# Re-tuning the planner of an attention-plus-MoE kernel: a larger reserve for DMA landings, and new order constants

## The chip, the cores and the metric

The kernel runs on one core of one Trainium2 chip. The metric is the device time of one execution in microseconds (us), lower is better. Its matrix engine is called PE here (PEld is its weight load), the vector engine DVE, the scalar (activation) engine ACT, the engine for memsets and cross-partition reductions POOL, and the queue that issues nearly all transfers SP.

## The reference

Eight batches of eight attention heads. Each sequence has 32 global and 512 local positions of 64 values. Global queries look at everything; local ones look at the global keys and at a band of 32 positions to either side. The attention output of all 4352 tokens then goes through a two-layer network with a Mish activation.

```python
s_g  = scale * q_g @ concat(k_g, k_l).T ;  out_g = softmax(s_g) @ v_all
s_ll = where(|i - j| <= 32, scale * q_l @ k_l.T, -1e9)
out_l = softmax(concat(scale * q_l @ k_g.T, s_ll)) @ concat(v_g, v_l)
x = concat(out_g, out_l) as (8 * 544, 512)
h = x @ w_in                 # 512 x 2048
g = h * tanh(log1p(exp(h)))  # Mish
return g @ w_out             # 2048 x 512
```

## The kernel before, in words

**Numbers as pairs.** Most matrix products run in 16-bit floats, with each operand split into a high and a low half, and three products (high-high, high-low, low-high) summed in PSUM. So most tiles come as a "hi" copy, made by ACT or DVE (line 347 on ACT, 349 on DVE), and a "lo" rest, which only DVE makes. The two weight matrices arrive as 64-bit floats in 32 half blocks of 512 KB. DVE rebuilds 32-bit floats from their bits in three instructions per half block (lines 426, 428, 435), PE squares them for a norm (`w_stat`, line 454, into the tile `w_s`), and a short chain over DVE, POOL and ACT turns the norm into a scale (`w_norm`, lines 461 to 474, tile `wp`, result `sw`). After that each of 16 weight blocks is split: hi by ACT or DVE, lo by DVE (line 486).

**Attention.** A unit is one batch `b`, one pair of heads `hp` and one quarter `t` of the sequence: 128 units. In each, PE makes two score tiles `s` (line 676 in 32-bit for the first eight head pairs, line 683 after that), DVE masks them and takes the row maximum (line 689), ACT exponentiates (line 698), ACT or DVE and then DVE split the result to `ph` (line 750). For batch 0 PE transposes it; from batch 1 on the DMA does (`pt<-ph`, line 509). Then PE multiplies by the values into `U` (line 767), whose normalised sum is `x` (line 777). The values reach the partitions where `U` needs them in seven small transfers per head pair (`va`, `vc`).

**Network.** There are 17 blocks of 256 tokens with 8 steps each. A step of the first product writes `h` (24 matmuls of 256 columns, line 899), ACT makes Mish out of it (`e`, line 942, with a table that must be loaded when the last function was an exponential), DVE splits it to `G` (lines 349 and 955), and a step of the second product adds it to `o` (12 matmuls of 512 columns, line 967). Two PSUM banks hold `h`, so a third step can start only when Mish has emptied the first.

**Who sets the order.** Each piece of work is a task with an engine (or a choice of two), a duration, what it reads and writes, and a priority. The class `Plan` simulates the five engines with these durations, always takes the task that can start first, and the simulated order is the order in which each engine's instructions are issued; nothing is reordered on the chip. A transfer's task is done, for the planner, at the time `served` at which its bytes have gone through, plus 400 ns, plus a reserve: `SPARE` when it is issued after the plan's time `SPARE_T`. Tasks of the weights get their due time as a place (`slot`) among the units: `CONV1`, `RATE1`, `CONV2`, `RATE2` for the conversions, `FIRST1`, `STEP1`, `FIRST2`, `STEP2` for the splits, `AHEAD_DMA` for the loads. `LEAD0`, `PACE` and `TAIL` say at which unit each network step is put; `LATE_*` postpone some loads and batch 1's preparation.

**Fillers.** The planner models that PE's clock is halved when the stretch of 3.4 us before had too few columns. Until the first `o` it therefore puts in matmuls that compute nothing which is used (line 1195, `w_s<-consts`, 256 columns). It does so where PE would wait at least `SLACK` longer than the filler takes, or where a debt stands: each task that uses few rows of the array adds its duration times `BOOST` to the debt, and a debt is paid in fillers whether PE would wait or not. In both cases it stops when the current stretch has `TARGET` columns.

Of the kernel before, what the change touches and what calls it, by code (L numbers as in the profile page):

```python
# [51 lines left out]
class Plan:  # L52
# [6 lines left out]
    DMA_IN, DMA_OUT, DMA_DEPTH = 1500, 400, 5500  # L59
    TICK, COLUMNS, PHASE = 10240 / 3, 3200, 0  # L60
    LOYAL = 800
    SLACK = 9.408
    TARGET = 5179.472
    SPARE_T = 148519.765
    BOOST = 0
    SPARE = 474.406
    TABLE = 1283

    def __init__(self):
# [75 lines left out]
    def order(self):  # L145
# [9 lines left out]
        start, done, on = [None] * N, [0] * N, [None] * N  # L155
        columns = {}
        served, spare, debt, last = 0, True, 0, 1
# [38 lines left out]
        for _ in range(N):  # L196
            t, pri, e, n, ns = min(c for c in map(first, free) if c)
            if any(tag == "o" for tag, _ in self.tasks[n][4]) and n != self.filler[0]:
                spare = False
            if e == PE and spare and done[self.filler[0]]:  # L200
                z, rows = max(free[PE], done[self.filler[0]] + self.HOP[DMA][PE]), self.tasks[n][6]
                while rows > last / 2 and columns.get(int((z + self.PHASE) / self.TICK), 0) < self.TARGET and (
                        debt > 0 and rows > 0.5 or tensor(z, self.filler[1], 1, False) + self.SLACK <= t):
                    z = tensor(z, self.filler[1], 1)
                    debt = max(0, debt - self.filler[1])
                    self.fill[n] = self.fill.get(n, 0) + 1
                t = max(t, z) if n in self.fill else t
                debt += ns * max(0, 1 - rows) * self.BOOST
                last = rows
            start[n], on[n] = t, e  # L210
            if e == ACT:
                self.table = self.tasks[n][7] or self.table
            for x, _ in self.tasks[n][0]:
                queue[x] = [c for c in queue[x] if c[1] != n]
            if e == PE:
                ns = tensor(t, ns, self.tasks[n][6]) - t
            if e == DMA:
                issue, ns = ns[:2]
                free[e] = t + issue + max(0, served - t - self.DMA_DEPTH)
                served = max(served, t + self.DMA_IN) + ns  # L220
                done[n] = served + self.DMA_OUT + (self.SPARE if t > self.SPARE_T else 0)
            else:
                free[e] = done[n] = t + ns
            for u in users[n]:
                left[u] -= 1
                if not left[u]:
                    enter(u)
# [17 lines left out]
def attn_mish_kernel(ctx: ExitStack, tc: tile.TileContext, qt, kt, qt0, kt0, mxs, vm, vg, qg, w1, w2, consts_in, out, w64):  # L245
# [80 lines left out]
    def bulk(kib):  # L326
        return dma(kib) + (BULK,)

# [664 lines left out]
        UNITS[:16] = sorted(UNITS[:16], key=lambda x: (x[2] // 2, x[1], x[2]))  # L993
    steps = [(blk, i) for blk in range(NBLK) for i in range(NF)]

    LEAD0 = 20.957
    PACE = 0.887
    TAIL = 14
    M1S = []
    for s in range(len(steps)):  # L1000
        at = int(LEAD0 + PACE * s) if s < 2 * NF else s + TAIL
        if s % NF == 0 and steps[s][0] < 2 * B:
# [136 lines left out]
                g_split(b + 1)  # L1139


    BULK = 4939.749
    LAG = 8
    ORDER = "k0 q0 m b k1 q1 w0 w1 g w3 w2 k2 q2 w4 w5 w6 w7 k3 q3 w8 w9 w10 w11 w12 w13 w14 w15"
    CONV1 = -2
    RATE1 = 1.119
    CONV2 = 0.367
    RATE2 = 1.486
    FIRST1 = 9.219
    STEP1 = 1.048  # L1150
    FIRST2 = 18.957
    STEP2 = 1.572
    AHEAD_DMA = 5.543
    LATE_K = 185.137
    LATE_L = 190.5
    LATE_B = 0
    LATE_V = 106.565

    def weights():
        for k in range(32):  # L1160
            at = CONV1 + RATE1 * k if k < 16 else CONV2 + RATE2 * (k - 16)
            if k >= 16:
# [22 lines left out]
    V.memset(pmax, 0.0)  # L1185
    for x in ORDER.split():
        a, n = x[0], int(x[1:] or 0)
# [94 lines left out]
```

## Time and profile before

| | |
|---|---|
| median of 3 runs | 954.24 us (954.09 to 954.46) |
| the profiled execution | 955.77 us, span 954.0 us |
| mean granted PE clock | 0.995 |
| PE busy | 919.7 us (96%) |
| DVE busy | 668.0 us (70%) |
| ACT busy | 629.0 us (66%) |
| DMA packets' time | 61.2% of 16 engines |

A row of the groups reads: line, engine, operation, output<-input, shape, count, then busy time and mean duration of one, then the idle time just before them. Matmul rows overlap, so their mean duration is longer than the distance between two of them; that distance is read from the chain of waits.

### The profile page before, as it was taken

The numbers are of one execution on the slowest core, as the hardware profiler recorded it, in microseconds if no ns is written. First come the engines' busy times: TensorE is split into PE (matmuls) and PEld (weight loads), VectorE is DVE, ScalarE is ACT, GpSimd is POOL, SyncE is SP. The second block draws the span as 40 slices with busy tenths as digits, with TensorE's granted clock in tenths as the row PEclk, the third lists the DMA queues.
The fourth block names the chain that finished last, engine by engine and source line by source line (L and its number), as shares of the span: only waits on it lengthen the run. The fifth ranks groups of instructions, "written<-read, shape, count | busy, mean of one in ns | idle before, by whom it ended". The sixth has DMA issues, their size and how long they took to land.

```text
span 954.0 us, 21026 instructions
## 1 busy us (share of the span) xinstructions
PE 919.7 (96%) x8181; PEld 641.5 (67%) x8181; DVE 668.0 (70%) x1771; ACT 629.0 (66%) x1284; POOL 16.2 (2%) x28
## 2 busy tenths in 40 slices
PE   7999999999999999999999999999999999999995
PEld 4666776557777777676777766677767776666663
DVE  6799988978999899767877777777766653222221
ACT  4557766778877898777886888687867881212110
POOL 2000000000000000000000000000000000000000
PEclk9999999999999999999999999999999999999998
DMA  9897446979998999756776576656765531000000
GB/s 305 266 292 219 117 143 150 203 154 241 242 250 194 263 217 197 160 125 142 168 169 129 138 164 161 131 142 148 167 120 110 94 77 24 23 2 23 1 23 23
DMA packets 214012, 141.04 MB, mean 148 GB/s; under 512 B 176664, under 2 KB 188184, under 8 KB 212888
## 3 DMA queue, kind: packets, MB, share of 16 engines
q1 hardware_dynamic: 213912, 139.69, 61.2%
q8 instruction: 64, 1.05, 0.5%
q14 instruction: 36, 0.29, 0.1%
HBM read 75.15 MB, written 8.91 MB: 88 GB/s over the span
## 4 chain that ended last, share of the span: by engine, by line
PE 75%; DVE 10%; DMA 8%; ACT 3%; SPq 2%; issue 2%; POOL 0%; DVEq 0%; ACTq 0%
PE h L899 31%; PE o L967 30%; DMA pt<-ph 5%; PE U L767 4%; PE s L683 3%; PE s L676 2%; PE g L807 2%; PE gu L856 1%; PE w_s L1195 1%; DVE W L428 1%; SPq L336 1%; DVE P L689 1%; DVE W L435 1%; SPq L509 1%; DVE ph L750 1%
## 5 line engine op out<-in xcount | busy, mean ns | idle before, releaser
L967 PE MATMUL o<-W,G 128*128 128x512 f16 x1632 | 390.9, 380 | 2.1 <-ACT W L347 1.1
L899 PE MATMUL h<-xh,W 128*128 128x256 f16 x2048 | 374.7, 273 | 0.1
L899 PEld LDWEIGHTS <-W 128*128 128x128 f16 x3264 | 311.0, 98 | 62.6 <-issue 6.0
L899 PE MATMUL h<-xl,W 128*128 128x256 f16 x1024 | 279.0, 272 | 0.0
L967 PEld LDWEIGHTS <-G 128*128 128x128 f16 x1632 | 156.8, 98 | 148.5 <-issue 5.8
L942 ACT ACTIVATE e<-h,c 128x512 f32<-128x512 f32 (+1 forms) x137 | 90.9, 682 | 124.8 <-PE h L899 118.8
L349 DVE TENSOR_SCALAR G<-e,c 128x512 f16<-128x512 f32 (+1 forms) x115 | 55.2, 480 | 149.1 <-ACT e L942 149.0
L698 ACT ACTIVATE P<-P,nm 128x192 f32<-128x192 f32 (+1 forms) x256 | 117.8, 461 | 48.0 <-DVE nm L689 45.0
L955 DVE SCALAR_TENSOR_TENSOR G<-e,c,G 128x512 f16<-128x512 f32 (+1 forms) x137 | 101.7, 743 | 2.3
L689 DVE CUSTOM_DVE_ANT_0 P<-s,consts 128x192 f32<-128x192 f32 (+1 forms) x256 | 90.7, 362 | 15.2 <-PE s L683 9.4
L750 DVE SCALAR_TENSOR_TENSOR ph<-P,ph 128x448 f16<-128x448 f32 (+1 forms) x112 | 65.0, 583 | 45.4 <-ACT ph L347 44.5
L942 ACT ACT_TABLE_LOAD x60 | 77.0, 1283 | 1.8 <-PE h L899 0.8
L698 ACT ACT_TABLE_LOAD x56 | 71.8, 1283 | 1.0
L767 PEld LDWEIGHTS <-pt 96*128 96x128 f16 (+1 forms) x1536 | 60.7, 97 | 14.7 <-DMA pt<-ph 9.6
L347 ACT ACTIVATE ph<-P 128x384 f16<-128x384 f32 (+1 forms) x108 | 58.7, 546 | 7.2 <-DMA pt<-ph 5.0
L767 PE MATMUL U<-va,pt 128*128 128x64 f16 (+1 forms) x768 | 55.1, 193 | 6.9 <-DMA pt<-ph 6.7
L767 PE MATMUL U<-vc,pt 96*128 96x64 f16 x768 | 54.9, 192 | 0.0
L683 PEld LDWEIGHTS <-qs 128*128 128x128 f16 x384 | 35.5, 98 | 23.1 <-issue 1.5
L698 ACT ACTIVATION_READ_ACCUMULATOR P<-P,nm 128x1 f32 x256 | 47.9, 187 | 0.0
L683 PE MATMUL s<-ks,qs 128*128 128x192 f16 (+1 forms) x192 | 42.7, 253 | 0.6 <-ACT gP L829 0.6
L829 ACT ACTIVATE gP<-g,gmx 64x288 f32<-64x288 f32 x64 | 30.3, 475 | 19.5 <-DVE gmx L824 19.4
L683 PE MATMUL s<-kl,qs 128*128 128x192 f16 (+1 forms) x192 | 42.6, 252 | 0.0
(125 smaller groups left out, 958.5 us busy)
## 6 DMA issues: line engine op xcount, KB each, us to landing
kraw<-in_kt SPq DMA_DIRECT2D x24, 640.0 KB, 4.7
kn_m<-in_mxs SPq DMA_DIRECT2D x24, 544.0 KB, 5.0
qraw<-in_qt SPq DMA_DIRECT2D x24, 512.0 KB, 4.5
out<-ob SPq DMA_DIRECT2D x34, 256.0 KB, 2.6
vraw<-in_vm SPq DMA_DIRECT2D x8, 1024.0 KB, 6.1
wraw<-in_w SPq DMA_DIRECT2D x16, 512.0 KB, 6.9
W<-in_w SPq DMA_DIRECT2D x16, 512.0 KB, 5.9
vc<-vf SPq DMA_DIRECT2D x32, 128.0 KB, 2.4
```

Of the source, the lines that this page charges most:

```text
L347: A.activation(out=dst, in_=src, func=AF.Copy, scale=c)
L349: V.tensor_scalar(dst, src, c, None, ALU.mult)
L683: T.matmul(X[s][:, :w], X[qs][:, h, t * 128:(t + 1) * 128], X[k][:, h, c0:c0 + w], start=(i == 0), stop=(i == 1))
L689: pl.add(DVE, 69 + 1.04 * w, lambda: V.tensor_tensor_reduce(out=X[P][:, h, :w], in0=X[s][:, :w], in1=mask[:, m0:m0 + w], scale=-SCALE, sca ...
L698: pl.add(ACT, 94 + 0.832 * w + 186, lambda: A.activation(out=X[P][:, h, :w], in_=X[P][:, h, :w], func=AF.Exp, bias=X[nm], scale=-1.0, accu ...
L750: pl.add(DVE, dve(n), lambda: V.scalar_tensor_tensor(p_part(X[ph], t, 1), p_src(X[P], t), PSC, p_part(X[ph], t, 0), ALU.mult, ALU.subtract ...
L767: T.matmul(X[u][:, t, h, :], X[pt][:k, p * 4 + h * 2 + c, :], X[vx][:k, t, vl, h * 64:(h + 1) * 64], start=(n == 0), stop=(n == 5))
L829: pl.add(ACT, 464, lambda part=part, c0=c0, c1=c1: A.activation(out=X[P][:, c0:c1], in_=X["g", b, hp, part][:64, 0:c1 - c0], func=AF.Exp, ...
L899: T.matmul(X[h][:, f * TB:(f + 1) * TB], wh(i, wl)[:, off:off + 128], X[x][:, d, o:o + TB], start=(n == 0), stop=(n == 11))
L942: chain(blk, i, ACT, 587, lambda a, z: A.activation(out=X[e][:, a:z], in_=hv(blk, i)[:, a:z], func=AF.Mish, bias=0.0, scale=X[c][:, 0:1]), ...
L955: chain(blk, i, DVE, 663, lambda a, z: V.scalar_tensor_tensor(gp(1, blk, i)[:, a:z], X[e][:, a:z], X["c", blk][:, 2:3], gp(0, blk, i)[:, a ...
L967: T.matmul(X[o], gp(g, blk, i)[:, f, t * 128:(t + 1) * 128], wh(8 + i, wl)[:, f * 512:(f + 1) * 512], start=(i == 0 and n == 0), stop=(i = ...
```

## The change

One rule and a set of constants change; no operation of the reference's computation is added or taken away.

```diff
-    SLACK = 9.408
-    TARGET = 5179.472
-    SPARE_T = 148519.765
-    BOOST = 0
-    SPARE = 474.406
+    RESERVE = 900
+    SLACK = 580.912
+    TARGET = 5641.608
+    SPARE_T = 42922.55
+    BOOST = 1.114
+    SPARE = 1474.111
...
-                done[n] = served + self.DMA_OUT + (self.SPARE if t > self.SPARE_T else 0)
+                done[n] = served + self.DMA_OUT + (self.RESERVE if t > 230000 else self.SPARE if t > self.SPARE_T else 0)
...
-    LEAD0 = 20.957
-    PACE = 0.887
-    TAIL = 14
+    LEAD0 = 18.646
+    PACE = 1.215
+    TAIL = 19
...
-    BULK = 4939.749
+    BULK = 5052.75
-    ORDER = "k0 q0 m b k1 q1 w0 w1 g w3 w2 k2 q2 w4 w5 w6 w7 k3 q3 w8 w9 w10 w11 w12 w13 w14 w15"
+    ORDER = "k0 q0 m b k1 w0 q1 w1 g w3 w2 q2 w4 k2 w5 q3 w6 w7 k3 w9 w10 w15 w11 w8 w13 w14 w12"
...
-    RATE2 = 1.486
-    FIRST2 = 18.957
-    STEP2 = 1.572
+    RATE2 = 1.396
+    FIRST2 = 24.578
+    STEP2 = 2.285
...
-    LATE_K = 185.137
-    LATE_L = 190.5
-    LATE_B = 0
+    LATE_K = 36.919
+    LATE_L = 293.152
+    LATE_B = 100.998
```

The reserve of a transfer is now 1474 ns when the plan issues it between 42.9 and 230 us, and 900 ns after that; it was nothing before 148.5 us and 474 ns after that. `DMA_OUT` (400 ns) comes on top in both. The fillers get a debt, and rise from 193 to 312; 287 of them stand ahead of the first `h`, where 192 did. All line numbers after line 61 are larger by one in the changed kernel. Four hi copies move from ACT to DVE, and ACT's table loads rise from 121 to 126.

How the order moves is shown at three places. The first is PE at the start: the score tiles of batch 0 (`s_0_0_t_head`), then before:

```order
L676 MATMUL s_0_0_0_0_110<-kn_0_0_93,qn_0_0_95 128x192
L676 MATMUL s_0_0_0_1_115<-kn_0_0_93,qn_0_0_95 128x192
L676 MATMUL s_0_0_1_0_121<-kn_0_0_93,qn_0_0_95 128x224
L676 MATMUL s_0_0_1_1_126<-kn_0_0_93,qn_0_0_95 128x224
L722 MATMUL T_0_0_0_133<-consts_65,P0_74 128x128 x4
L676 MATMUL s_0_0_2_0_145<-kn_0_0_93,qn_0_0_95 128x224
```

and now:

```order
L677 MATMUL s_0_0_0_0_109<-kn_0_0_93,qn_0_0_95 128x192
L677 MATMUL s_0_0_0_1_114<-kn_0_0_93,qn_0_0_95 128x192
L677 MATMUL s_0_0_1_0_121<-kn_0_0_93,qn_0_0_95 128x224
L677 MATMUL s_0_0_1_1_128<-kn_0_0_93,qn_0_0_95 128x224
L1196 LDWEIGHTS consts_65
L1196 MATMUL w_s_97<-consts_65 128x256
```

Thirteen fillers now stand before the first transposition `T`; before, the first filler came after 16 norm matmuls of `w_stat`, behind the first scores of head pair 1.

The second place is PE at the first step of the second product, `o_0_0`. The names are `h_block_step`. Before:

```order
L899 MATMUL h_1_2_1831<-xl_0_501,W_72 128x256
L899 LDWEIGHTS W_72
L899 MATMUL h_1_2_1831<-xh_0_451,W_72 128x256
L967 LDWEIGHTS G_0_1536
L967 MATMUL o_0_0_1893<-W_72,G_0_1536 128x512
```

and now:

```order
L900 MATMUL h_0_7_1864<-xl_0_571,W_72 128x256
L900 LDWEIGHTS W_72
L900 MATMUL h_0_7_1864<-xh_0_520,W_72 128x256
L968 LDWEIGHTS G_0_1593
L968 MATMUL o_0_0_1920<-W_72,G_0_1593 128x512
```

On DVE the first split of a second-matrix block (line 486, now 487) is followed by one reduction and the next split; before, 25 other instructions lay between those two. Eleven whole steps of `h` (264 matmuls) stood ahead of the first `o`; now eight (192) do. The rest of PE's work ahead of it is the same in number, apart from the fillers.

The third place is ACT around the norm of the second weight matrix (`wp_1`; the names `e_block_step` are Mish, `vf` and `vgf` the values of batch 1, and `W` the hi copy of a weight block). Before:

```order
L586 ACTIVATE vgf_1_1778<-vgraw_1_203,sv_1_1756 128x128
L347 ACTIVATE vf_1_0_1782<-vraw_1_929,sv_1_1756 128x4x128
L347 ACTIVATE vf_1_1_1785<-vraw_1_929,sv_1_1756 128x4x128
L942 ACTIVATE e_0_7_1803<-h_0_7_1700,c_0_1100 128x512
L347 ACTIVATE G_3_1776<-e_0_7_1803,c_0_1100 128x512
L942 ACTIVATE e_1_0_1824<-h_1_0_1763,c_1_1557 128x512
L347 ACTIVATE G_4_1828<-e_1_0_1824,c_1_1557 128x512
L467 ACT_TABLE_LOAD
L467 ACTIVATE wp_1_1735<-wp_1_1735 128x1
L468 ACT_TABLE_LOAD
L468 ACTIVATE wp_1_1735<-wp_1_1735 128x1
L347 ACTIVATE W_72<-W_72,sw_70 128x1024
```

and now:

```order
L943 ACTIVATE e_0_3_1716<-h_0_3_1634,c_0_952 128x512
L830 ACT_TABLE_LOAD
L830 ACTIVATE gP_1_0_1750,gs_1_0_1751<-g_1_0_0_1595,gmx_1_0_1647 64x288
L468 ACT_TABLE_LOAD
L468 ACTIVATE wp_1_1725<-wp_1_1725 128x1
L699 ACT_TABLE_LOAD
L699 ACTIVATE P2_76,sums_1_1_1761<-P2_76,nm_1_1_0_0_1731 128x192
L469 ACTIVATE wp_1_1725<-wp_1_1725 128x1
L587 ACTIVATE vgf_1_1767<-vgraw_1_257,sv_1_1753 128x128
...
L348 ACTIVATE W_72<-W_72,sw_70 128x1024
L943 ACT_TABLE_LOAD
```

The norm's two functions stand ahead of batch 1's values now, and ahead of the fifth Mish step of block 0 where they followed the first step of block 1.

More of the change, by code (lines that the diff above doesn't have):

```diff
@@ L1139, in slot @@
                 g_split(b + 1)
-    BULK = 4939.749
+    BULK = 5052.75
     LAG = 8
-    ORDER = "k0 q0 m b k1 q1 w0 w1 g w3 w2 k2 q2 w4 w5 w6 w7 k3 q3 w8 w9 w10 w11 w12 w13 w14 w15"
-    CONV1 = -2
-    RATE1 = 1.119
-    CONV2 = 0.367
-    RATE2 = 1.486
-    FIRST1 = 9.219
-    STEP1 = 1.048
-    FIRST2 = 18.957
-    STEP2 = 1.572
-    AHEAD_DMA = 5.543
-    LATE_K = 185.137
-    LATE_L = 190.5
-    LATE_B = 0
-    LATE_V = 106.565
+    ORDER = "k0 q0 m b k1 w0 q1 w1 g w3 w2 q2 w4 k2 w5 q3 w6 w7 k3 w9 w10 w15 w11 w8 w13 w14 w12"
+    CONV1 = 0.868
+    RATE1 = 0.869
+    CONV2 = 0
+    RATE2 = 1.396
+    FIRST1 = 11.002
+    STEP1 = 1.007
+    FIRST2 = 24.578
+    STEP2 = 2.285
+    AHEAD_DMA = 4.214
+    LATE_K = 36.919
+    LATE_L = 293.152
+    LATE_B = 100.998
+    LATE_V = 116.143
     def weights():
```

## The prediction

> **What bounds the kernel now.** I read the page's busy shares first, then PE in stages of the span, then the fillers in the same stages, and last what DVE and PE waited for in each.
>
> ```profile
> span 954.0 us, 21026 instructions
> PE 919.7 (96%) x8181; PEld 641.5 (67%) x8181; DVE 668.0 (70%) x1771; ACT 629.0 (66%) x1284; POOL 16.2 (2%) x28
> ```
>
> PE's useful work is the same in both kernels. So the time is that work, plus fillers, plus PE's gaps, plus what follows its last matmul, and only the last three can change. The stages (columns: busy us of PE, PEld, DVE, ACT, POOL; clock; DMA):
>
> ```profile
> core 0: us, PE busy (x) PEld busy (x) DVE busy (x) ACT busy (x) POOL busy (x), PEclk, DMA share, GB/s
> 0.00:32.30 32.30, 24.62 (x97) 15.25 (x98) 23.80 (x75) 12.06 (x36) 6.79 (x13) 1.00 0.86 278
> 32.30:100.10 67.80, 61.22 (x653) 45.04 (x651) 60.72 (x167) 45.81 (x117) 0.49 (x1) 1.00 0.89 259
> 100.10:133.40 33.30, 32.83 (x296) 27.75 (x296) 31.51 (x77) 24.23 (x46) 0.71 (x2) 1.00 0.40 116
> 133.40:142.30 8.90, 6.88 (x35) 3.69 (x34) 6.78 (x23) 5.48 (x7) 1.06 (x1) 0.81 0.57 176
> 142.30:230.00 87.70, 84.69 (x767) 53.52 (x766) 74.64 (x188) 61.99 (x144) 0.35 (x1) 1.00 0.83 180
> 230.00:800.00 570.00, 565.50 (x5364) 400.43 (x5362) 434.30 (x1182) 454.73 (x900) 6.85 (x10) 1.00 0.71 160
> 800.00:944.00 144.00, 143.96 (x982) 95.80 (x980) 35.50 (x62) 24.61 (x36) 0.00 (x0) 1.00 0.03 12
> 944.00:954.00 10.00, 0.00 (x0) 0.00 (x0) 0.75 (x1) 0.04 (x1) 0.00 (x0) 0.65 0.17 52
> ```
>
> The same stages for `w_s` alone (fillers and norm matmuls):
>
> ```profile
> 0.00:32.30 32.30, 8.25 (x49) 0.00 (x0) 1.00 0.86 278
> 32.30:100.10 67.80, 30.80 (x249) 0.29 (x1) 1.00 0.89 259
> 100.10:133.40 33.30, 2.50 (x25) 0.29 (x1) 1.00 0.40 116
> ```
>
> Until 100 us PE has 14.3 us of gaps, and 39 us go to `w_s`: DVE sets the pace there (60.72 of 67.80 us). From 100.1 us, the first `h`, to 133.4 us PE is full. It loses 2.0 us around the first `o`, more for a halved clock, then 3.0 us to 230 and 4.5 us to 800. After that nothing is lost until the last 10 us, the same tail in both kernels. So the change can act at four places: before the first `o`, right behind it, up to 230 us, and up to 800 us.
>
> **The change part by part.**
>
> *The three deferred steps.* The order shows eight instead of eleven `h` steps ahead of the first `o`, other useful work being equal. Two pieces of the chain give what a step costs:
>
> ```profile
> 259.27 1.31 PE h L899 x12
> 262.41 2.59 PE o L967 x12
> ```
>
> A step has 24 matmuls: 2.62 us; three are 7.86 us, which must now be done later. At an unchanged start of the first `o` the end would move by **+7.9 us**. The start, however, hangs on DVE and ACT:
>
> ```profile
> 124.45 0.29 DVE L461 CUSTOM_DVE_ANT_0 wd<-w_s,consts 128x128 f32<-128x128 f32 x1 [0.18 <-PE w_s L454]
> 131.15 1.28 ACT L467 ACT_TABLE_LOAD   x1
> 134.19 0.15 DVE L353 TENSOR_SCALAR wp<-wp 128x1 int32<-128x1 int32 x1 [1.70 <-ACT wp L468]
> 135.95 1.28 DVE L486 SCALAR_TENSOR_TENSOR W<-W,sw 128x1024 f16<-128x1024 f32 x1 [0.91 <-ACT W L347]
> 135.97 0.38 PE L967 MATMUL o<-W,G 128*128 128x512 f16 x1 [1.08 <-ACT W L347]
> 137.29 4.08 PE L967 MATMUL o<-W,G 128*128 128x512 f16 x11 [0.94 <-DVE W L486]
> ```
>
> The second norm starts at 124.45 us and its scale is used from 134.8 us on, because ACT reaches the logarithm only at 131.15 us. Now that function stands ahead of the fifth Mish step, so the scale comes early, and the two waits of DVE (1.70 and 0.91 us) fall away. DVE's rows ahead of the first split of a second-matrix block are the same as before by line and count, less three `G` lo's:
>
> ```profile
> L955 DVE SCALAR_TENSOR_TENSOR G<-e,c,G 128x512 f16<-128x512 f32 (+1 forms) x137 | 101.7, 743 | 2.3
> ```
>
> That is 3 x 0.743 = 2.2 us. Waits and rows together make 4.8 us. But the order now has a table load (1.28 us in the rows above) and an exponential between the norm's two functions, and Mish waits behind the hi copy, so I count 3.0 of them: the first `o` at about 133.0 us. The part comes to 7.9 - 3.0 = **+4.9 us**. Its lower end is what DVE can save at most, its waits between 10 and 136 us:
>
> ```profile
> DVE P L689 <- PE s L676: 3.3, 4, 1.4
> DVE x L777 <- PE U L767: 3.2, 1, 3.2
> DVE vmx L524 <- DMA vraw<-in_vm: 2.5, 1, 2.5
> DVE wp L353 <- ACT wp L468: 1.7, 1, 1.7
> DVE W L486 <- ACT W L347: 0.9, 1, 0.9
> ```
>
> Without the one for `vraw`, whose load keeps its place, they are 9.1 us; with the 2.2 us the part would be 7.9 - 11.3 = -3.4. The upper end is no earlier start at all, +7.9, or more if fillers delay DVE (a rival).
>
> *The fillers.* 119 more, each 109 ns (the 24 matmuls of a step have the same 256 columns): 13.0 us. Up to 133.4 us PE was busy for 24.62 + 61.22 + 32.83 = 118.7 us; less the 7.9 of the deferred steps and with these 13.0 it is 123.8 us in 133. They fit, and I cost them at nothing; DVE's work is the cover. But the debt's fillers stand in front of score tiles without regard to a gap. If all were uncovered they would cost 13.0 us. On the other side they may bring something:
>
> ```profile
> 25.11 2.55 PE L1195 MATMUL w_s<-consts 128*128 128x256 bf16 x11
> 59.08 1.69 PE L1195 MATMUL w_s<-consts 128*128 128x256 bf16 x14
> ```
>
> Eleven fillers took 2.55 us at 25 us, fourteen only 1.69 us at 59 us: PE ran at half speed at first. With thirteen of them from the fifth instruction on it should be fast sooner. This helps only where DVE waits for PE, at most the 3.2 us for `U` and part of the 3.3 us for score tiles, and is inside the lower end above. The Trainium skill ("TensorE: Matmul & The Clock Gate", Part 1) says that one busy window of about 3.4 us releases the clock; by that rule the fillers free it some 20 us earlier and the sum would be up to 3.2 us lower; the rows fit the rule, but do not show when thirteen fillers suffice.
>
> *Right behind the first `o`.* The stage from 133.4 to 142.3 us has a granted clock of 0.81, and eleven `o` matmuls took 4.08 us where 11/12 of 2.59 are 2.37: 1.7 us, and the wait of 0.94 us for DVE's lo is on top. In the changed order only one reduction lies between the first two splits on DVE, so I take the wait to go; whether the clock stays up depends on PE's gaps just before. I take **-2.0 us** (0 to -2.7).
>
> *The reserve, 142 to 230 us.* What PE waits for there, then what its weight loads wait for, then the same from 230 to 800 us:
>
> ```profile
> PE U L767 <- DMA pt<-ph: 2.9, 3, 1.1
> PEld L767 <- DMA pt<-ph: 4.1, 3, 1.6
> PE U L767 <- DMA pt<-ph: 3.9, 5, 1.6
> PEld L767 <- DMA pt<-ph: 5.5, 6, 1.9
> ...
> DMA to landing us min/median/max: 3.0/3.3/8.0
> ```
>
> Nearly the whole gap of the stage (3.0 us) is `U` waiting for a transposed `pt` that landed late. The plan now puts `U` at least 1.0 us later against its `pt` (1474 less 474), with other matmuls between. Three waits of at most 1.1 us on PE: almost all go. I take **-2.5 us**; bounds -3.0, and +1.0 if the deferred `h` steps make new waits for the late Mish.
>
> *The reserve, 230 to 800 us.* Five waits, 3.9 us, of the 4.5 us lost. The reserve grows by 0.426 us, so five times that, 2.1 us, is the most that is moved out of the way by it alone; a landing of 8.0 us against a median of 3.3 is far outside it. I take **-1.5 us**, bounds -4.5 (every gap of the stage) and +1.5 (the late landings meet another order as badly).
>
> *Copies and tables.* Four hi copies go to DVE, five table loads of 1.28 us come on ACT, 6.4 us in all. From 230 us on PE is full (565.50 of 570) while ACT is busy 454.73; this hides them. Without cover they would cost 6.4 us.
>
> **Sum.** 4.9 - 2.0 - 2.5 - 1.5 = -1.1 us, from 955.77 us of the profiled execution to 954.67. That execution is 1.53 us above the median of the runs, so by the median: **953.1 us**. About 0.2% (1.9 us) is what a measurement of this kernel can tell from no change; this forecast lies inside it.
>
> **The rivals.**
>
> *A: faster, 949.9 us.* The early fillers wake PE's clock, and DVE's waits for `U` and scores shrink by half (-3.2 of 6.5), all else as above: 953.1 - 3.2. For it: eleven fillers in 2.55 us, and DVE at 60.72 of 67.80, so each DVE wait counts. Against: the plan puts the first `x` right behind its last conversion, so some wait for `U` stays. The rule of the Trainium skill above ("TensorE: Matmul & The Clock Gate", Part 1) speaks for this case.
>
> *B: slower, 958.3 us.* The debt's fillers lie on the path. Most score tiles of batch 0 come behind some of them on PE, which takes them in order; DVE's row maximum follows the scores, and DVE sets the pace. 95 of the 119 stand ahead of the first `h`: 10.4 us; if half is uncovered, 5.2 us come to the sum: 953.1 + 5.2 = 958.3. It decides from the point where DVE's waits for `s` exceed the 3.3 us of now. Against: DVE has conversions to do in between, and PE has 14.3 us of gaps to fill.
>
> *C: the reserve does not do what it says, 956.1 us.* If the late landings are later than the reserve covers, the 2.5 fall to 1.0 and the 1.5 to 0: 953.1 + 3.0 = 956.1. For it: the landing of 8.0 us against a median of 3.3. Against: the single waits from 142 to 230 us were at most 1.1 us on PE, about what the reserve grows by.
>
> **How the numbers follow.** The forecast (951.0 to 955.2) has 0.45, A 0.23, B 0.22, C 0.10. The range holds 8 in 10: **949.0 to 958.5**. It takes in the times of A, B and C; A's bound of 7.9 - 11.3 with every late landing avoided, and B's 13.0 us, are left out as the outer 2 in 10. Faster by over 0.2% (below 952.3): A and 0.13 of the forecast, 0.36. Within: 0.32 of the forecast and 0.06 of C, 0.38. Slower (above 956.1): B and 0.04 of C, 0.26.
>
> **What would show it.** First `h` between 100 and 103 us and first `o` at 133: the three steps' term is right. PE's gap from 142 to 230 us falls from 3.0 to about 0.5; from 230 to 800 us from 4.5 to 3. Fillers take 109 ns each from about 10 us on if the clock wakes. It is wrong if the first `o` starts later than 136 us, if DVE's waits for `s` grow, if `U` waits for `pt` as before, or if PE has gaps between 142 and 230 us that Mish ends.

## The result

The changed kernel takes 963.33 us (median of 4 runs, 961.92 to 963.97) beside 954.35 us of the kernel before on the same chip: a ratio of 1.0087, 95% interval 1.0072 to 1.0102. It is 9 us slower. The forecast was 953.1 us with a range of 949.0 to 958.5, so the measured time lies outside the range, and on the other side of the kernel before.

The profiled execution of the changed kernel is the shortest of its four, 961.92 us; that of before was 955.77 us. So the two traces hold 6.15 of the 9 us. The head of the changed kernel's page:

```profile
span 960.1 us, 21263 instructions
PE 924.8 (96%) x8300; PEld 645.0 (67%) x8300; DVE 671.6 (70%) x1775; ACT 632.5 (66%) x1285; POOL 16.8 (2%) x28
```

Its stages, in the columns of the prediction's table (the borders are the changed kernel's first `h`, first `o` and last matmul):

```profile
0.00:32.30 32.30, 24.20 (x175) 16.62 (x176) 25.59 (x77) 12.07 (x36) 7.24 (x13) 1.00 0.91 292
32.30:100.30 68.00, 63.12 (x681) 46.55 (x679) 62.03 (x169) 46.89 (x117) 0.38 (x1) 1.00 0.79 254
100.30:131.60 31.30, 29.47 (x255) 23.61 (x253) 29.56 (x77) 26.22 (x46) 1.26 (x2) 1.00 0.51 142
131.60:142.30 10.70, 10.70 (x91) 6.13 (x88) 10.32 (x21) 4.24 (x6) 1.08 (x1) 1.00 0.62 141
142.30:230.00 87.70, 85.53 (x757) 55.15 (x755) 72.51 (x192) 65.51 (x145) 0.35 (x1) 1.00 0.83 182
230.00:800.00 570.00, 561.66 (x5333) 397.06 (x5334) 434.15 (x1179) 452.19 (x901) 6.48 (x10) 1.00 0.72 158
800.00:950.30 150.30, 150.13 (x1024) 99.90 (x1021) 36.87 (x65) 25.34 (x37) 0.00 (x0) 1.00 0.03 11
950.30:960.10 9.80, 0.00 (x0) 0.00 (x0) 0.61 (x1) 0.00 (x0) 0.00 (x0) 0.75 0.18 54
```

The first `h` starts at 100.3 us (100.1 before), the first `o` at 131.6 (136.0 before), and behind it PE is full at a granted clock of 1.00, where it had 6.88 of 8.90 us at 0.81. From 142.3 to 230 us PE gains 0.84 us (85.53 against 84.69). From 230 to 800 us it loses 3.84 (561.66 against 565.50). That loss lies in one piece. The stage from 230 to 350 us, first of the kernel before, then of the changed one:

```profile
230.00:350.00 120.00, 119.44 (x1150) 84.54 (x1148) 109.44 (x294) 103.61 (x206) 2.07 (x5) 1.00 0.97 233
```

```profile
230.00:350.00 120.00, 115.21 (x1135) 81.50 (x1136) 108.72 (x291) 96.17 (x200) 2.21 (x5) 1.00 0.97 226
```

What PE waited for in this stage of the changed kernel (us in total, times, longest):

```profile
PE U L768 <- DMA pt<-ph: 4.3, 3, 1.7
PE gu L857 <- DMA gpt<-gph: 0.7, 1, 0.7
PE h L900 <- ACT e L943: 0.6, 1, 0.6
```

In the kernel before `U` waited 0.5 us for `pt` there. The DMA engines are at a share of 0.97 in both kernels. In the chain of work that ended last, these three waits of `U` end with transpositions that took 6.74, 8.21 and 5.83 us from the start of their issue to their landing. The first of them in that chain, SP's issues up to it (start, duration, what), and the wait on PE:

```profile
224.16 6.74 DMA pt<-ph
```

```profile
221.00 1.74 SPq L510 DMA_TRANSPOSE pt<-ph  x1
222.80 0.76 SPq L337 DMA_DIRECT2D kn_m<-in_mxs  x1
223.65 0.41 SPq L337 DMA_DIRECT2D out<-ob  x1
224.16 1.48 SPq L510 DMA_TRANSPOSE pt<-ph  x1
```

```profile
230.95 0.26 PE L768 MATMUL U<-va,pt 128*128 128x64 f16 x3 [1.71 <-DMA pt<-ph]
```

It stands in SP's queue behind another transposition and a bulk load. Its own issue is short (1.48 us), but it lands 6.74 us after its start, where the quickest take 3.0 us. The transpositions of `pt` from 142 to 350 us in the changed kernel (min/median/max, from issue to landing):

```profile
DMA to landing us min/median/max: 3.0/5.0/7.4
```

In the kernel before the median is 4.2 us there. Some issues are slow as well, so that what stands behind them on SP comes later. This one took 3.26 us, where the shortest took 1.23, and the trace shows no wait of SP in it:

```profile
289.95 3.26 SPq L510 DMA_TRANSPOSE pt<-ph  x1
```

From 142 to 350 us 13 of 67 transpositions took over 2 us to issue in the changed kernel, 7 of 69 before. Part of these times is SP waiting for another engine: of the longest, 4.29 us from 208.28 us on, the waits put 3.2 us down to PE. DVE waited for the bulk loads themselves, too (230 to 350 us; 0.2 us in the kernel before):

```profile
DVE mx L555 <- DMA kn_m<-in_mxs: 3.7, 3, 2.3
```

To place losses in kernels of different order I also count PE's **lost time**: the time up to a point less the durations of all matmuls but fillers begun by then (`h` 109.4 ns, `o` 216.5, `U` 27.8, scores 88.7 and 98.9, `g` 93.1, fitted on stretches without gaps). It is good to 1 or 2 us. By 142.3 us it is 57.0 before and 57.8 changed; it grows by 4.7 and 9.5 until 350 us, and by 3.3 and 3.9 until 800. The differences, 0.8 + 4.8 + 0.6 = 6.2 us, are nearly the 6.15 us by which the two profiles differ. PE's busy time above, with a gain of 0.84 and a loss of 3.84 us from 142.3 us on, shows 2.4 us less of it.

### The profile page after: what moved, and what is told of

Read it like the earlier page. It is cut to its first block, busy times and chain, and to the rows that moved or that the text cites. A ratio compares the mean times of both kernels' runs of the same rounds, so it can differ in the third digit from the quotient of the medians.

```text
span 960.1 us, 21263 instructions
## 1 busy us (share of the span) xinstructions
PE 924.8 (96%) x8300; PEld 645.0 (67%) x8300; DVE 671.6 (70%) x1775; ACT 632.5 (66%) x1285; POOL 16.8 (2%) x28
## 4 chain that ended last, share of the span: by engine, by line
PE 58%; DVE 17%; ACT 10%; DMA 8%; issue 4%; SPq 1%; ACTq 0%; DVEq 0%
PE o L968 24%; PE h L900 24%; PE U L768 3%; DMA pt<-ph 3%; ACT L943 3%; DVE G L956 2%; ACT P L699 2%; PE s L684 2%; DVE P L690 2%; DMA kn<-in_kt 2%; ACT e L943 2%; DVE kl L622 1%; DVE G L350 1%; PE s L677 1%; DMA gpt<-gph 1%
## 5 line engine op out<-in xcount | busy, mean ns | idle before, releaser
L751 DVE SCALAR_TENSOR_TENSOR ph<-P,ph 128x384 f16<-128x384 f32 (+1 forms) x112 | 65.3, 583 | 56.2 <-ACT ph L348 55.9
L348 ACT ACTIVATE ph<-P 128x384 f16<-128x384 f32 (+1 forms) x112 | 61.2, 546 | 16.8 <-DMA pt<-ph 14.5
L1196 PE MATMUL w_s<-consts 128*128 128x256 bf16 x312 | 45.6, 279 | 0.0
```

The source lines that it names most:

```text
L348: A.activation(out=dst, in_=src, func=AF.Copy, scale=c)
L751: pl.add(DVE, dve(n), lambda: V.scalar_tensor_tensor(p_part(X[ph], t, 1), p_src(X[P], t), PSC, p_part(X[ph], t, 0), ALU.mult, ALU.subtract ...
L1196: pl.filler = (len(pl.tasks), mm(1, 262), lambda: T.matmul(X["ws"][:, 256:], ident.bitcast(BF16)[:, :128], ident.bitcast(BF16), start=fres ...
```

## The experiments

Theory R is the prediction's view turned round: the larger reserve itself made the order worse. D, M and E put it down to the due times, the places of the Mish steps, or the early part. Theory S came out of the traces: SP's queue slips where bulk loads fill the DMA engines; the order of before happens to have little waiting at these slips, and another order has more. Each run stands beside the kernel before on its own chip. The diff ahead of the prediction leaves out that `CONV1`, `RATE1`, `CONV2`, `FIRST1`, `STEP1`, `AHEAD_DMA` and `LATE_V` change too; they belong to the groups of e2 and e4. Results of all runs (the last three columns are the lost time by 142.3 us, and its growth to 350 and from there to 800 us):

| run | us | beside before | by 142.3 | to 350 | to 800 |
|---|---|---|---|---|---|
| before (profiled) | 954.4 | | 57.0 | 4.7 | 3.3 |
| changed | 963.3 | +9.0 | 57.8 | 9.5 | 3.9 |
| e1 changed, reserve undone | 973.6 | +19.0 | 58.0 | 19.0 | 5.8 |
| e2 changed, due times undone | 962.9 | +8.3 | 59.7 | 8.2 | 4.4 |
| e3 changed, Mish places undone | 965.5 | +10.9 | 66.7 | 8.2 | -1.3 |
| e4 changed, early part undone | 959.3 | +4.7 | 59.6 | 5.1 | 3.0 |
| e5 reserve alone | 968.5 | +13.7 | 62.3 | 6.5 | 7.5 |
| e6 early part alone | 963.0 | +8.2 | 61.3 | 8.1 | 2.2 |
| e7 due times alone | 957.8 | +3.0 | 55.6 | 9.1 | 2.7 |
| e8 Mish places alone | 969.2 | +14.5 | 56.4 | 16.1 | 5.8 |
| e9 changed, light loads | 954.7 | -0.3 | 59.2 | 2.0 | 3.4 |
| e10 before, light loads | 949.0 | -6.1 | 55.6 | 2.2 | 0.0 |
| e11 = e1, light loads | 967.9 | +12.8 | 58.0 | 14.6 | 4.9 |
| e12 = e8, light loads | 960.9 | +5.9 | 55.5 | 10.2 | 4.7 |
| e13 reserve, 148 to 230 us alone | 956.2 | +2.4 | 56.7 | 7.2 | 3.2 |
| e14 reserve 900 from 230 us alone | 953.7 | 0.0 | 55.8 | 5.8 | 1.4 |
| e15 reserve 1474 from 230 us alone | 952.6 | -1.2 | 56.9 | 5.0 | 2.9 |
| e16 reserve, 43 to 148 us alone | 962.2 | +7.7 | 60.5 | 5.1 | 4.2 |
| e17 changed, no reserve until 148 us | 970.5 | +15.9 | 58.5 | 16.5 | 4.1 |
| e18 reserve 2200 from 230 us alone | 953.0 | -1.6 | 56.2 | 4.4 | 2.2 |

### One part of the change undone

```diff
 # e1
-    SPARE_T = 42922.55
-    SPARE = 1474.111
-    RESERVE = 900
+    SPARE_T = 148519.765
+    SPARE = 474.406
+    RESERVE = 474.406
```

> The changed kernel with the reserve of before alone (474.406 ns from 148.5 us of the plan to its end); all other constants are the new ones. The changed kernel took 963.3 us and lost 5.9 of its 136 us of PE between 214 and 350 us; the kernel before took 954.4 us. Theory R (the larger reserve turned the order there against the transposes): the time falls to 952 to 957 us, and PE is busy for 134.5 us or more of the 136. Theory D (the due times of loads and preparation, LATE_K, LATE_L, LATE_B, LATE_V, crowd SP's queue and the DMA engines there) and theory M (the later places of the Mish steps, PACE and TAIL, pull the attention's work of DVE and SP forward): the stall stays, 961 to 966 us, perhaps 1 us more, since the reserve no longer covers single late landings.

973.6 us, ratio 1.0203 (1.0188 to 1.0218): against theory R. In the changed kernel the reserve saves 10 us. What PE waited for from 142 to 214 us without it:

```profile
PE U L768 <- DMA pt<-ph: 5.7, 3, 4.1
PE h L900 <- ACT e L943: 2.7, 1, 2.7
...
```

The stretch right behind the longest of these waits (the clock is the column behind POOL):

```profile
185.00:189.00 4.00, 3.74 (x26) 2.74 (x27) 3.90 (x15) 1.71 (x4) 0.83 (x1) 0.50 1.16 153
```

Behind the wait of 4.1 us PE's granted clock was 0.50 for these 4 us, so this wait cost more than its length.

```diff
 # e2
-    LATE_K, LATE_L, LATE_B, LATE_V = 36.919, 293.152, 100.998, 116.143
+    LATE_K, LATE_L, LATE_B, LATE_V = 185.137, 190.5, 0, 106.565
 # e3
-    LEAD0, PACE, TAIL = 18.646, 1.215, 19
+    LEAD0, PACE, TAIL = 20.957, 0.887, 14
 # e4: SLACK, TARGET, BOOST, ORDER, BULK, AHEAD_DMA, CONV*, RATE*, FIRST*, STEP* of before
```

> The changed kernel with LATE_K, LATE_L, LATE_B and LATE_V of before (185.137, 190.5, 0, 106.565 in place of 36.919, 293.152, 100.998, 116.143); all else new. Theory D: 952 to 957 us, PE busy for 134.5 us or more between 214 and 350 us, and SP, which issued DMAs for 62.4 of the 68 us from 283 to 351 us in the changed kernel and for 49.3 us in the kernel before, comes back to about 50. Theories R and M: 961 to 966 us, the gaps of U on pt stay about 6 us in that stage.

962.9 us, 1.0089 (1.0072 to 1.0105): theory D falls by the time. The waits did move, against what was expected under R and M. PE from 142 to 350 us:

```profile
PE h L900 <- ACT e L943: 2.3, 2, 2.0
PE gu L857 <- DMA gpt<-gph: 1.9, 1, 1.9
PE U L768 <- DMA pt<-ph: 0.6, 1, 0.6
...
```

`U` waits 0.6 us for `pt` in place of 4.6, other waits have grown in its place, and the stage still loses 8.2 us.

> The changed kernel with LEAD0, PACE and TAIL of before (20.957, 0.887, 14 in place of 18.646, 1.215, 19); all else new. This puts the Mish steps from the third block on five places earlier against the attention, so less of DVE's and SP's attention work falls before 350 us. Theory M: 952 to 957 us, and at the most 1.5 us of PE's gaps remain between 214 and 350 us. Theories R and D: 961 to 966 us. Whatever the theory, the first o should come later than the changed kernel's 131.6 us if more h steps precede it again (each is 2.62 us).

965.5 us, 1.0119 (1.0097 to 1.0141): theory M falls, and `U` still waits 4.4 us for `pt` from 142 to 350 us. The first `o` came at 144.9 us, later, as the last sentence expected.

> The changed kernel with the early part of before: fillers (SLACK, TARGET, BOOST), order and distance of the loads (ORDER, BULK, AHEAD_DMA) and the places of the weights' conversion (CONV, RATE, FIRST, STEP); reserve, due times and Mish places stay new. Theory E (the different start leaves DVE or the buffers in another state, and the stall at 214 to 350 us follows from it): 952 to 957 us. Theories R, D and M: the stall stays, and the kernel loses what the early part brought, about 1 us by the loss at 217 us (before 60.1 us of PE's time not spent on useful work, changed 59.1): 962 to 967 us.

959.3 us, 1.0054 (1.0037 to 1.0071): a gain of 4 us, less than theory E's. It lies between 142 and 350 us, where the loss falls from 9.5 to 5.1 us, nearly the 4.7 of the kernel before, and `U` waits 0.4 us for `pt`; the start is worse by 1.8. So the stage's loss goes with the new early part, as theory E has it, but no single part carries the 9 us.

### One part alone in the kernel before

The same four groups of constants, each put into the kernel before.

> The kernel before with the new reserve alone (1474 ns from 42.9 us of the plan, 900 ns from 230 us); all other constants as before. Undoing the reserve in the changed kernel cost 10.2 us (973.6 against 963.3). Theory R2 (a larger reserve keeps U away from late landings in any order): the kernel before has 7.5 us of PE gaps behind the first o, the reserve takes a part of them: 949 to 953.5 us. Theory S (the order of before is one in which the slips of SP's queue happen to fall where nothing waits; any other order meets them): 957 to 968 us, with U waiting for pt between 142 and 350 us for 4 us or more.

968.5 us, 1.0164 (1.0131 to 1.0197). Theory R2 falls. S's range ends just below, and `U` waits 3.0 us for `pt` from 142 to 350 us, not the 4 or more that S asked for. The same reserve that saves 10 us in the changed kernel costs 13.7 in the one before, by the lost time 5.3 of it ahead of 142.3 us, 1.8 up to 350 and 4.2 behind.

> The kernel before with the new early part alone (fillers, order and distance of the loads, places of the weights' conversion). Its undoing in the changed kernel gained 4 us (959.3 against 963.3). Theory E2 (the new early part is what costs, whatever the rest): 957 to 960 us. Theory S (any other order meets the slips of SP's queue): 957 to 968 us as well, but with the loss at U waiting for pt between 142 and 350 us and not before the first o. Neither: 953 to 955 us.

963.0 us, 1.0105 (1.0082 to 1.0127), half of the loss ahead of 142 us and half behind, where `U` waited 4.2 us for `pt`. So neither E2's nor S's account explains it alone.

> The kernel before with the new LATE_K, LATE_L, LATE_B and LATE_V alone. Undoing them in the changed kernel moved nothing (962.9 against 963.3). If the parts acted by themselves and summed, this run would be at 954 to 955 us. Theory S: 957 to 968 us, by waits of U for pt between 142 and 350 us.

957.8 us, 1.0040 (1.0022 to 1.0058): +3.0, though undoing it moved nothing. The time lies at the lower end of S's range, but not by S's waits: from 142 to 350 us `U` waits 2.2 us for `pt`, `s` 2.8 us for DVE and `h` 2.2 us for Mish.

> The kernel before with the new LEAD0, PACE and TAIL alone. Undoing them in the changed kernel cost 2.2 us (965.5 against 963.3), so if the parts acted by themselves and summed, this run would be at 951 to 953 us. Theory S: 957 to 968 us, by waits of U for pt between 142 and 350 us.

969.2 us, 1.0169 (1.0147 to 1.0191), where the sum of parts promised a gain. `U` waits 6.5 us for `pt` from 142 to 350 us, as S has it, and the time is 1.2 us above S's range. Each part alone is slower by 3 to 14.5 us; the four sum to 39 us, and together they are 9. The parts don't add: together the constants make one order.

### The same orders with light loads

```diff
+    def few(b, i, n):
+        return n if (b, i) == (2, 0) else n // 8
-        pl.add(DMA, dma(640), lambda: load(X["kraw", b, hp], kt[b, hp]), new=[("kraw", ("kraw", b, hp))])
+        pl.add(DMA, dma(640), lambda: load(X["kraw", b, hp].rearrange("p a n -> p (a n)")[:, :few(b, hp, 2 * KW)], kt[b, hp][:, :few(b, hp, 2 * KW)]), new=[("kraw", ("kraw", b, hp))])
 # the same for qraw and kn_m; of vraw one quarter from batch 2 on; their tiles are allocated once
```

These four kernels leave out seven eighths of `kraw`, `qraw` and `kn_m` of batches 2 to 7 (but for the first of each kind) and three quarters of `vraw`. The planner's costs are untouched, so every instruction keeps its place.

> The changed kernel, every instruction in its place, but the bulk loads of batches 2 to 7 (kraw, qraw, the kn_m of the norms, vraw) move only an eighth of their bytes (vraw a quarter); the first of each kind stays whole. Left out are seven eighths of these inputs (three quarters of vraw), so what is computed from them is not the reference's. Theory S (SP's queue slips where bulk loads fill the DMA engines, an issue then takes up to 4.3 us, and U waits for pt): no issue of a transpose takes over 2 us between 196 and 350 us, U's waits for pt there (about 5 us) go, and the time falls to 955.5 to 959 us. If the losses come from DVE's or ACT's order instead, the traffic does not matter: 961.5 to 964 us.

954.7 us, 8.6 less than with full loads, a little below the range of theory S. The two stages in the changed order with light loads:

```profile
142.30:230.00 87.70, 87.70 (x794) 57.44 (x792) 76.05 (x201) 65.98 (x146) 0.72 (x2) 1.00 0.66 127
230.00:350.00 120.00, 119.19 (x1179) 85.29 (x1178) 111.84 (x295) 100.43 (x212) 1.69 (x4) 1.00 0.61 122
```

What PE still waited for from 230 to 350 us (lines are larger by ten in the kernels with light loads):

```profile
PE h L910 <- ACT e L953: 0.6, 2, 0.3
PE gu L867 <- DMA gpt<-gph: 0.3, 1, 0.3
```

No `U` waits for `pt` any more from 142 to 350 us, and PE's idle time there falls from 2.17 + 4.79 to 0.81 us. Four of 67 transpositions still took over 2 us to issue (the longest 2.86, of which the waits put 2.8 down to PE), so that number of the expectation was not met. What changes most is the time from issue to landing, from a median of 5.0 to 3.2 us:

```profile
DMA to landing us min/median/max: 3.0/3.2/5.4
```

DVE's wait for `kn_m` is gone as well. That the loads are behind the loss of this stage is shown; how much of it goes through late landings, slow issues or DVE's own wait is not separated.

> The kernel before with the same lighter bulk loads (an eighth of the bytes, vraw a quarter; the rest of these inputs is left out), every instruction in its place. Theory S: its order lost only 3 us to U's waits for pt between 142 and 350 us, and one of 1.8 us at 692 us, so it gains 1 to 4 us: 950 to 953.5 us. It stays ahead of the changed kernel with lighter loads by 4 us or more only if the changed order has losses that do not come from the loads.

949.0 us, 0.9947 (0.9929 to 0.9964): 6.1 less, more than expected, since lost time behind 350 us goes as well (3.3 to 0.0; `U` waits 0.6 us for `pt` there in place of 3.4). From 142 to 350 us the two orders now lose the same, 2.0 and 2.2: the whole difference of that stage comes from how each order meets the bulk loads. But over the whole kernel 5.8 us between the two orders remain, where it was 9.0 with full loads: by the expectation's last sentence the changed order has losses that do not come from the loads. By the count they are 3.6 ahead of 142.3 us and 3.4 behind 350. Behind 350 PE waits 2.6 us for `ob` and `gP` in the changed order with light loads, 0.5 us for `gP` in the order of before.

> The changed kernel with the reserve of before (973.6 us, of which 17 us are lost between 142 and 350 us, 6.7 of them by U waiting for pt and 3.5 by h waiting for Mish), and the bulk loads of batches 2 to 7 cut to an eighth of their bytes (vraw to a quarter), the rest of these inputs left out. Theory S: late landings are the origin of most of it, the Mish waits included (what waits for a load on DVE and ACT holds up Mish behind it): 956 to 963 us, so that the reserve is worth under 4 us once the loads are light, where it was worth 10.2 us. If DVE's and ACT's order lose it by themselves: 970 to 974 us.

967.9 us: 5.7 less, and of the 19.0 us lost between 142 and 350 us 14.6 remain. Theory S does not explain this one, and the other range is missed as well. PE from 142 to 350 us waited for:

```profile
PE h L910 <- ACT e L953: 6.4, 3, 2.8
PE U L778 <- DMA pt<-ph: 1.4, 3, 0.6
PE o L978 <- DVE W L497: 1.4, 1, 1.4
```

With full loads (e1) `h` waited 3.5 us for Mish there and `U` 6.7 for `pt`. In front of the wait of 2.66 us that ends at 183.9 us ACT makes Mish behind a row of exponentials, and PE's order has no other work at that point.

> The kernel before with the new LEAD0, PACE and TAIL (969.2 us, 14.7 us lost between 142 and 350 us) and the bulk loads of batches 2 to 7 cut to an eighth of their bytes (vraw to a quarter), the rest of these inputs left out. Theory S: 953 to 961 us. If the new places of the Mish steps lose it by themselves, whatever the loads do: 966 to 970 us.

960.9 us: 8.3 less, the upper end of S. From 142 to 350 us `U` waits 0.4 us for `pt` where it was 6.5 with full loads (e8), but `h` waits 5.0 us for Mish where it was 1.2. So in these two orders (e11, e12) there are two losses: `U` behind late transpositions, which goes with the loads, and `h` behind Mish, which then comes forward.

### The reserve by its stages

```diff
 # e13, kernel before:  SPARE 474.406 -> 1474.111 from 148.5 to 230 us of the plan, RESERVE = 474.406
 # e14, kernel before:  RESERVE = 900 from 230 us of the plan; e15: 1474.111; e18: 2200
 # e16, kernel before:  1474.111 from 42.9 to 148.5 us of the plan, 474.406 from there
 # e17, changed kernel: SPARE_T = 148519.765
```

> The kernel before with one constant and no other changed: the reserve is 1474 ns in place of 474 from 148.5 to 230 us of the plan, and 474 again behind it. The order is the same as before up to 155.6 us of the plan. This is the prediction's term for 142 to 230 us alone (-2.5 us, bounds -3.0 and +1.0), so by the prediction 951 to 952.5 us. Theory P (in this stage SP, DVE and the DMA engines have nothing left to put ahead, so a reserve only moves U and all behind it, and the plan itself then waits): 957 to 963 us, PE's gaps between 196 and 250 us grow by 3 us or more.

956.2 us, 1.0025 (1.0014 to 1.0036): slower. The stretches from 142 to 196 and 196 to 250 us in the kernel before:

```profile
142.00:196.00 54.00, 51.70 (x461) 32.35 (x459) 47.21 (x112) 36.12 (x81) 0.35 (x1) 1.00 0.80 170
196.00:250.00 54.00, 53.30 (x508) 35.65 (x507) 46.38 (x133) 44.69 (x103) 0.37 (x1) 1.00 0.90 203
```

and with the reserve of this stage alone, the third row being the time right behind a new wait:

```profile
142.00:196.00 54.00, 53.33 (x470) 32.97 (x469) 47.68 (x112) 37.42 (x84) 0.35 (x1) 1.00 0.73 169
196.00:250.00 54.00, 51.46 (x481) 34.85 (x480) 44.62 (x134) 36.96 (x95) 0.37 (x1) 0.97 0.92 200
...
219.20:222.00 2.80, 2.73 (x25) 2.22 (x26) 2.60 (x13) 1.75 (x7) 0.00 (x0) 0.60 1.74 255
```

The new wait, in PE's order of time:

```profile
219.27 0.26 PE L768 MATMUL U<-va,pt 128*128 128x64 f16 x3 [2.53 <-DMA pt<-ph]
```

The reserve does what the prediction said until 196 us (1.63 us gained), and then the new order has one `U` that waits 2.53 us, more than the reserve holds, with the clock at 0.60 behind it. Theory P has the place right, but not the size: it is one wait, and the run ends below P's 957 us and well above the 952.5 us that the prediction's term allows.

> The kernel before with the reserve at 900 in place of 474 ns from 230 us of the plan on, nothing else changed; the order is the same as before up to 242 us of the plan. This is the prediction's term for 230 to 800 us alone (-1.5 us, bounds -4.5 and +1.5): 952 to 954 us, with the waits of U for pt from 350 us on (0.64, 0.81, 1.16 and 1.81 us before) smaller. Theory S (any new order meets the slips of SP's queue): 957 us or more, by waits between 250 and 400 us. Theory P: no loss, since behind 390 us SP, DVE and the DMA engines have time to spare; what is lost is lost between 250 and 390 us.

953.7 us, 1.0001 (0.9986 to 1.0016): no gain. From 230 to 800 us four waits of `U` for `pt` remain, 2.7 us in place of 3.9.

> As the run with 900 ns from 230 us of the plan, but with 1474 ns, about what the single waits of U for pt behind 350 us need (the longest was 1.8 us, under a reserve of 474). If a reserve avoids late landings where the engines have time to spare: no wait of U for pt behind 400 us, and 950.5 to 953.5 us. If the order between 250 and 390 us decides: 956 us or more.

952.6 us, 0.9987 (0.9974 to 1.0000): at the edge of a gain. Three waits of `U`, 1.6 us, remain, 0.2 of them behind 400 us.

> The kernel before with the reserve at 2200 ns in place of 474 from 230 us of the plan on, nothing else changed. At 900 the time was 953.7 and at 1474 952.6 us beside 953.8 of before. If a reserve avoids late landings where SP and DVE have time to spare, no U waits for pt behind 390 us, and the time is 951 to 953 us, at least not above 1474's. If a large reserve pushes attention work into other work's place, new waits (U for x, o for ob, h for e) appear and the time is back at 954 us or more.

953.0 us, 0.9980 (0.9971 to 0.9990): a little faster than before, with the lowest ratio of all kernels here that do the whole work. Its stage from 230 to 800 us:

```profile
230.00:800.00 570.00, 567.79 (x5379) 402.57 (x5377) 437.51 (x1184) 449.13 (x898) 7.78 (x10) 1.00 0.71 160
```

All that PE waited for in it:

```profile
PE s L684 <- ACT gP L830: 2.1, 3, 0.8
```

No `U` waits for `pt` there; before, five did, for 3.9 us. So a late reserve does remove these waits, and the larger the reserve, the fewer stay (900, 1474 and 2200 ns leave 2.7, 1.6 and 0 us; `U` waited up to 1.6 us under a reserve of 0.47). In time 1474 and 2200 ns can't be told apart: their intervals overlap.

> The kernel before with the reserve at 1474 ns from 42.9 to 148.5 us of the plan and at 474 from there on (before: none until 148.5), nothing else changed. The reserve from 148.5 to 230 us alone cost 2.4 us and from 230 us on nothing, while the whole of it cost 13.7 us. If the parts sum, this one costs about 11 us: 963 to 966 us. By the profile of the whole reserve (5.3 us more lost before the first U of batch 1) it is about 5 us: 957 to 960 us, and the rest is the new order behind it meeting the loads. If it costs nothing: 953 to 955 us.

962.2 us, 1.0084 (1.0066 to 1.0101). This lies between the expectation's two ranges. By 142.3 us 3.5 us more are lost, the longest piece in front of the first `o`:

```profile
PE o L968 <- ACT W L348: 2.4, 1, 2.4
```

So more than half of what the whole reserve costs in the kernel before comes from its earliest part (7.7 of 13.7; the parts sum to 10.1).

> The changed kernel with the reserve starting at 148.5 us of the plan in place of 42.9 (474 becomes 1474 there as in the change, 900 from 230 us); all else new. All of the reserve undone made it 973.6 us, 10.2 more. If the early reserve is what the rest of the changed constants were chosen for: 968 to 975 us, with h waiting for Mish behind the first o. If the reserve behind 148.5 us brought the 10.2 us: 960 to 965 us.

970.5 us, 1.0167 (1.0153 to 1.0181): in the changed kernel the same earliest part saves about 7 us. Without it PE waits for Mish from 142 to 214 us:

```profile
PE h L900 <- ACT e L943: 3.9, 1, 3.9
```

In the old order the early reserve costs 7.7 us, in the new one it saves about 7: its worth depends on the rest of the constants.

## Why the prediction was wrong, step by step

**Three deferred steps (+4.9) and right behind the first `o` (-2.0): right in kind, the second in part by luck.** The first `h` was to stand between 100 and 103 us and the first `o` at 133; they stand at 100.3 and 131.6, and the half clock is gone. Together they were to cost 2.9 us. By the lost time at 142.3 us it is 0.8 in the two profiles; six executions that start in the order of before (before, e10, e13, e14, e15, e18) have 55.6 to 57.0, mean 56.4, and two in the changed order (changed, e9) 57.8 and 59.2, so about 2.1. The half clock was no fixed property of the old order, though: of these six executions, whose matmuls run in the same order until then, three (before, e13, e15) have 0.81 from 133.4 to 142.3 us, and three (e10, e14, e18) have 1.00. The term was read from one execution.

**The fillers at nothing: right.** With 95 more of them ahead of it the first `h` is at the same time (100.3 and 100.1 us). Rival B is out: DVE's waits for scores did not grow. What DVE waited for from 10 to 132 us in the changed kernel:

```profile
DVE x L778 <- PE U L768: 3.0, 3, 2.5
DVE W L427 <- DMA wraw<-in_w: 2.0, 1, 2.0
DVE wp L354 <- ACT wp L469: 1.5, 2, 1.3
...
```

The waits for `s` (3.3 us) have left this list. Rival A's premise holds too: thirteen fillers took 2.79 us, the next nine 1.16, 129 ns each, so the clock is free from about 11 us.

```profile
7.24 2.79 PE L1196 MATMUL w_s<-consts 128*128 128x256 bf16 x13
10.97 1.16 PE L1196 MATMUL w_s<-consts 128*128 128x256 bf16 x9
```

No run changes the fillers alone. The early clock bought no time: the wait for `U` is still 3.0 us, a wait of 2.0 us for `wraw` is new, and DVE sets the pace as before.

**The reserve, 142 to 230 us (-2.5): half right.** `U` waits 0.4 us for `pt` there in place of 2.9, as forecast. But `gu` waits 1.0 us for `gpt` now, and PE gains 0.84 us in place of 2.5. Alone (e13) this reserve even costs 2.4 us, by one new late landing.

**The reserve, 230 to 800 us (-1.5): this step failed.** By PE's busy time it measured +3.84 us, 4.23 lost up to 350 us and 0.38 gained behind. I counted five waits of the old trace, took off the growth of the reserve, and bounded the loss at +1.5, "the late landings meet another order as badly". Three things were wrong. First, only the reserve stood in that term, while ORDER, the due times and the places of the Mish steps move the order there too; I had no term for a new order as such. The runs price it: between 142 and 350 us each of the other three parts alone loses 3.4 us or more beyond the 4.7 of before (the reserve alone 1.8, with 5.3 lost ahead of it). Second, I took the late landings for scatter that a reserve absorbs. The larger ones belong to the order. The first of the waits of the kernel before, in that kernel and in e15, e18 and e14, which share its order up to there:

```profile
166.73 0.26 PE L767 MATMUL U<-va,pt 128*128 128x64 f16 x3 [1.10 <-DMA pt<-ph]
```

```profile
166.76 0.26 PE L768 MATMUL U<-va,pt 128*128 128x64 f16 x3 [1.22 <-DMA pt<-ph]
```

```profile
166.61 0.26 PE L768 MATMUL U<-va,pt 128*128 128x64 f16 x3 [1.79 <-DMA pt<-ph]
```

```profile
166.63 0.26 PE L768 MATMUL U<-va,pt 128*128 128x64 f16 x3 [2.21 <-DMA pt<-ph]
```

Four executions, four times the same `U` late by 1.1 to 2.2 us, landing within 0.15 us of the same time. (The second wait of that order, at 189 us, came back in three of the four.) An order made under a larger reserve gets its own late landings, and PE met three of them between 230 and 350 us. Third, even in the old order the reserve of 900 ns brought 0.0 us (e14), not 1.5: it shortened the waits and removed one of five.

That the bulk loads are behind them is shown (e9): in the changed order `U`'s waits between 142 and 350 us go with the loads, and there both orders then lose the same. Rival C named this direction ("later than the reserve covers") and priced it at 3.0 us, by the old order's waits. Which of the new constants brings the late landings into this stage is not settled: without the new early part (e4) they go, without the new due times (e2) they go but the time stays, without the new reserve (e1) the loss is twice as large.

**Copies and tables at nothing: not quite.** From 230 to 800 us PE waits 3.3 us for ACT (1.3 for `ob`, 1.3 for `gP`, 0.7 for Mish), where 0.6 for `gP` stood before. These 2.7 us more take the place of waits for `pt` behind 350 us, which fell from 3.4 to 0.7. No run shows whether the copies and table loads bring them, or the order.

**What stays open.** The profiles hold 6.15 of the 9 us; the other 2.8 lie in the scatter of executions. The 5.8 us by which the two orders with light loads still differ were followed to waits for ACT behind 350 us alone, not ahead of 142 us. Why the order without the reserve (e1, e11) lets Mish fall so far behind was seen, not tried.

## What to carry to other kernels

Where a planner writes out the whole order, price a change of its constants first as a new order: look for the stage in which several queues are full at once (here 230 to 350 us: the DMA engines at 0.97, DVE busy for 109 of 120 us), and let the range hold what a new order may lose there, some 5 us here, before any gain from the constant's own meaning. A long wait that is seen in a trace of a fixed order can belong to that order (one came back in four executions of four), so a margin has to cover its full length, and a margin makes a new order with waits of its own; here it paid only behind the crowded stage. Constants that were chosen together are not to be priced one by one: the early reserve cost 7.7 us with the old ones and saved about 7 with the new.

## What the runs showed of the hardware

PE's clock fell to half behind some idle times of little more than 2 us. In e14 the wait of 2.21 us was followed by

```profile
167.00:170.40 3.40, 3.40 (x21) 2.17 (x18) 3.40 (x5) 2.86 (x4) 0.00 (x0) 0.52 1.12 290
```

while in e18 the same `U` waited 1.79 us and the clock stayed at 1.00; nor did it move behind the 1.71 us in the changed kernel. But it did not fall behind each of them. In e8 PE waited 2.15 us for Mish, and the clock stayed at 1.00:

```profile
111.78 0.27 PE L900 MATMUL h<-xh,W 128*128 128x256 f16 x1 [2.15 <-ACT e L943]
```

```profile
111.80:115.20 3.40, 3.40 (x36) 3.09 (x36) 3.40 (x8) 0.83 (x2) 0.00 (x0) 1.00 0.64 175
```

Nor did it behind 2.14 us in e12 and 2.31 us in e7, while it did behind 2.02 us in e2 and 2.03 us in e6. So near 2 us the length of one wait does not decide, and these runs do not show what does. Where it fell in e14, the wait cost, by an estimate from the row above, some 1.7 us on top (3.4 us at half clock). The Trainium skill ("TensorE: Matmul & The Clock Gate", Part 1) says that gaps above about 3.4 us bring the half clock back; in these runs 2.02 us brought it once, and the measurement decides for this kernel.

From issue to landing a transposition of `pt` took 5.0 us (median, 142 to 350 us) in the changed kernel, with the DMA engines at a share of 0.91, and 3.2 us with light loads at 0.63; in the order of before it was 4.2 and 3.2 us. The shortest issue on SP took 1.23 us, and one in which the trace shows no wait of SP took 3.26 us.
